# K and Q of a sliding-window attention: masked while they leave PSUM, or copied first and masked in place

## The chip, the cores and the metric

The kernel runs on one core of a Trainium2 chip. The metric is the device time of one execution in microseconds. Five engines work from queues of their own: PE (TensorE) multiplies, DVE (VectorE), ACT (ScalarE) and POOL (GpSimd) do the elementwise work, and SP issues nearly all DMAs. They wait for each other through semaphores.

## The reference, cut to what matters

Two kinds of block run twice in turn on x of 2048 rows by 512 columns: attention with 32 heads of 16 columns and a window of 256 rows, and an MLP over the rows.

```python
def _A_ref(x, wqkv, wo):            
    q, k, v = ...                   # x @ wqkv, split into heads
    scores = einsum("bhqd,bhkd->bhqk", q, k) * (Dh ** -0.5)
    mask = (idx[:, None] - idx[None, :] >= 0) & (idx[:, None] - idx[None, :] < W)
    scores = where(mask, scores, -1e9)
    p = softmax(scores)
    return einsum("bhqk,bhkd->bhqd", p, v)... @ wo

def _B_ref(x, w1, b1, w2, b2):
    u = gelu(einsum("bsd,sf->bdf", layernorm(x), w1) + b1)
    return transpose(einsum("bdf,fs->bds", u, w2) + b2)

x = x + _A_ref(layernorm(x), ...); x = x + _B_ref(layernorm(x), ...)   # twice
```

## The kernel before

**Work.** A layer's attention goes through four blocks Q of 512 rows. For each block and each group t of 128 columns (8 heads), `project` (L521 to L530) makes K, Q and V: four 128x512 matmuls into one PSUM bank. Each (Q, t) then has nine steps m. A step is a score product (L684, cells of 64x64 in PE), an exp on ACT that writes the weights P to `p_sb` (L695), products with `edge` that mask the window's ends in P (L712, on DVE or POOL), and the product with V (`emit_pv`, L733) some steps later. There are 288 steps in the two layers. The MLP is two large products, L855 (u) and L928 (y); parts of both are placed among the attention steps.

**Masks of K and Q.** The score product works on several heads at once, so K and Q are kept in two copies each, with rows of other heads set to zero. K goes to `k_sb` with the two copies interleaved in runs of 32 columns, by the two-column mask `half`; Q goes to `q_sb` as two copies of 512 columns by `even`. `masked` (L532 to L544) does this straight from the bank: on DVE as one product of 1024 columns (L537), whose inputs are the bank in PSUM and the mask in SBUF, or on ACT as two activations with a scale (L542). The bank is held until this is done. The very first K and Q (t = 0 of the first block) come in halves of 256 columns (`first_half`), each masked in the same way.

**V.** V is copied out of its bank (L358 or L360), transposed (L601) and spread into `v_all` by a product of two SBUF operands (L586, on DVE, POOL or ACT). LayerNorm is L460 to L494, the inverse of the softmax sums L759 to L765, their spreading L777, the output product L653.

**Order.** Nothing is scheduled when the kernel runs. The program makes 2537 operations, each with the engines that could do it and a cost in ns. `ORDER` (L28) then gives, for each engine, the list of operations that it performs, in order, each named by two letters that number the operations as they are made. `BANKS` gives the one of two PSUM banks, 6 and 7, that each of the 200 "misc" products uses: projections, output products, parts of u and y. `Plan.needs` works out which semaphores each operation waits for. Each engine goes through its list strictly, so an operation that waits holds all behind it.

**Start.** SP loads x, the weights of K and Q in quarters, and V's weights. PE first multiplies an identity by itself as a warm-up (`warm`, L446: one operation is ten 128x128 matmuls, `WARM` = 10 operations), six of them at once, one after the first two transposes, three among the first scores.

Of the kernel before, what the change touches and what calls it, by code (L numbers as in the profile page):

```python
# [10 lines left out]
P = 128  # L11
# [3 lines left out]
WARM = 10  # L15
# [14 lines left out]
AuAvAwAxAyAzBLBJA0BPBRBNBTBXBVDTB1CeCuA1A2CjCoBpCyCcC3C9D1A3CnDEDKCxBtC2DODXC8DkDDDeDJDNDmDVDbBxDsDxB5DBD4DiD9DrGsEKECDwEFFZD3EPD8EBEaEJGQEOETEjEeEyEp  # L30
EuGiE3EiE8EoEtFBE2FJE7FOF2FVFAFIFcFEFxFNFSF4HlF9FbGCFwGIF1F8GMGBGTHYGdGHGLGSGWGlICGpGvHLG2GkGoG9G7HCGuG1HGIQHOG5HBHFHVHNHSHeHaHiHrI0HyHdH6HhHqHxH-HuII
H5H+INKmIcIHIMIgIkIoIVIsKUIxIfIjI6JpI-IrIwJVH1JaI5I+JiJCJmJEJuJZJ1JfJyJ6JdKwJlJ+JtJxKLJ5LpKPJ9KXLbKhKKKOKpMFKtKWKaKzK-K6KoLBKsKyK5LGLPLKK9LFLSNILYLJLh
NSLmLRLVLuNLL1LgL9LlLdMCLtL0MKL8MBLxMJMOMPMdNBMlMhMWMpNwMtMgMkMxL4M5MsMwM+NgNEM4M9NNNQNXNDNdMSNKNnNUNtNaN1NcNmN5OOOGNsN0OKO+OTN4OFOJOeOQOXOiOnOpOhOtPm
O0OmO6NqPBOsOzPFM0O5PKPSQYPAPEPfPJPPPZPVPtPYPePjPNP4PyNkPcQAPiPsQHPoPxP3QRP-O3QGQbQKQVQoQkQUQaQfRXP7QvQeQ1Q-Q5QjQuQ0RDORRKQ4Q+RORHQERURcRRRNRhRTRbRgRm
RlRzR0QsSuR3R4R5SxSyS0SrS1SvS3SwSGS6S7SDS4S2SVSJSsSRSNS8S5StSlSmSzSnS9TRTFTBTNTSTHTDTOTdTVThTZTaTeTWSoTiSpSqS-TLTJT1TwT7T2T8UAUBTxUpUOUdUXUZUqUTUVUkU2
UbUeU6UlUiVbUPVMVCVKWdVVVQWeU+VeVjYXVGYYVoVvVUVsXyXzWiVdV0ViV4VnVuVzWAWNV9WPV3V-WHWEWyXRWZWUXAWlWLWqZgXBWvW3WTWYWkXkYrW8WpXNWuZWXWW2W7XGXbX7XgXVXaXfXp
YQXuX4aFYAXoYFXtZvYMX3X-YEYJYTaGYmYta2YyYSYlY3YqYxY8adZHZAa3Y2Y7Y-ZZZGZKZRbgZdZjZEbhZqZxZYcDZ2ZcZiZpZ6Zta-aCaNZ-Z1aaZ5aBaKaWaQaqaVaZajaia8apaxaSa7aybK
cGbFbdcHbZbEbJbSdRbqbucbbybNbcb7blcAambtbxcTb6b-cYdjcgcFcXckatcscdcweNc4cjcrc8bmdJcvc3c7dIdNdMdUb1eZdedmcndTdXdrczdxd4d9dld-dqdwd3eEgAeId7eQemeWeDeHef
duejePeTerfDeze7eeebeifAfIeqeyeufNe6e-fbfHfMfUfffjfngjfrfvfegXf3fifqfuf9e2gDf2gIiDgQf8gCgHgNgUh0gcgggLgogTgbgfgsfQg5gngrg9hchIg4hTfyg8hEhMhXheighChihp
hshthWhwh3hbhhhFh7hohviAiSiIh2h6iPhGiWh-iFiaiTikiOiVipiLiZivijioi3iuidi2i-i+jCjJjQjNkRjTjXjgj4jcjojMiyjujSjWjbjyjnjtjxj8jkj3kDkAkHjlkKkOkWi7kGkbkNkVka  # L40
kgkfktkui8kLkxkykzlrlslulolllmlvlplAl0lxk9l1lylPltlDlzlLlHl2lwlqlnlflglhmBl9l-mLl3mMmbmTmUmHl7mImcmPmQlimXljlkmYl5mFmDmjm1msmkmnmwmom2mxmtm5m6nCm+m-nH
# [13 lines left out]
AjAiBMBQBSBUBYAtB2CfAmArCkCpCzAsC4C+CdDFDLBuDPDYDfDnDcByDtDyB6D+D5GtEDELB8EQEbEkEUEVEqEvE4E9FCFKFPFWFdFFFyF5F+GDGJGNGUGeGmGqGwG3G+HDHHHPHWHfHjHsHzH7IA
IJIOIdIhIpItIyI7JAJWA4JbJjJnJvJzJhJ7J-KMKQKYKiKqKuK0K7LCLHLLLTLZLiLnLvL2L+MDMLMQMeMiMqMuMyM6M-NFNONYNeNoNuN2N6OHOLOUOfOjOqOuO1O7PCPGM1PTPLPgPaPuPkPzP5
# [214 lines left out]
def bass_interleave_layers__sliding_block__mixer_token_mlp__prompt_kernel(  # L271
# [23 lines left out]
    with es:  # L295
# [49 lines left out]
        def dve(fn, work, prio, **kw):  # L345
            return plan.op({DVE: (work, fn)}, prio=prio, **kw)
# [716 lines left out]
```

## Time and profile before

| | |
|---|---|
| median of 3 runs | 492.03 us (491.97 to 492.04) |
| the profiled execution | 492.09 us |
| its span, first to last instruction | 490.3 us |
| granted TensorE clock | 1.00 |
| first exp | 12.2 us |
| matmuls of warm-up | 100 |
| ACT's idle time that ended with a score product | 23.8 us in 47 waits |
| POOL's idle time that ended with an exp | 99.0 us in 65 waits |

The page gives the busy time of each engine, the chain of work that ended last (followed back from the last instruction to whatever released each one), and groups of equal instructions: line, engine, operation, output and inputs, shape, count, then total busy us and mean ns, then idle time before them and what ended it. A line of the chain has its start, its duration and the instruction. Neighbouring instructions of one engine overlap a little, so two durations may add to more than the time that passes.

### The profile page before, as it was taken

How to read it: one execution, taken by the hardware profiler on the slowest of the kernel's cores; microseconds unless marked ns; L12 is line 12 of the kernel's file. 1: busy time of each engine (PE TensorE's matmuls, PEld its weight loads, DVE VectorE, ACT ScalarE, POOL GpSimd, SP SyncE). 2: the span in 40 equal slices, each digit the busy share in tenths (PEclk: the TensorE clock that was granted, in tenths of full speed). 3: DMA queues.
4: the chain of work that ended last, by engine and by line, in shares of the span. 5: the costliest groups of instructions: out<-in, count | busy, mean ns of one | idle time of the engine just before them, and what ended most of it. 6: DMA issues, size and time to landing. Idle time of an engine off the chain costs nothing.

```text
span 490.3 us, 17141 instructions
## 1 busy us (share of the span) xinstructions
PE 467.3 (95%) x7614; PEld 255.4 (52%) x7706; DVE 337.4 (69%) x710; ACT 319.8 (65%) x391; POOL 196.3 (40%) x362
## 2 busy tenths in 40 slices
PE   8989989999999999999999999999999999999997
PEld 6544555565555444444455555655556544444444
DVE  7999988988878550256878677999978745220214
ACT  5989989999989202404769898989999830440000
POOL 4989886444622210021439253645674220000000
DMA  7533159200105872240116300240020666080833
GB/s 215 100 77 90 40 115 97 70 6 25 50 6 153 237 175 76 75 132 19 31 16 170 51 27 4 39 101 8 24 70 4 197 188 171 0 226 19 228 107 118
DMA packets 83465, 43.58 MB, mean 89 GB/s; under 512 B 18752, under 2 KB 82368, under 8 KB 83392
## 3 DMA queue, kind: packets, MB, share of 16 engines
q1 hardware_dynamic: 79520, 42.48, 33.1%
q0 software_dynamic: 3872, 0.02, 1.8%
q8 instruction: 60, 0.98, 0.9%
q14 instruction: 13, 0.11, 0.1%
HBM read 32.51 MB, written 2.10 MB: 71 GB/s over the span
## 4 chain that ended last, share of the span: by engine, by line
PE 77%; DVE 14%; ACT 4%; issue 3%; POOL 1%; POOLq 0%
PE ps L855 19%; PE ps L928 18%; PE ps L526 12%; PE ps L684 11%; PE ps L733 9%; PE ps L653 4%; ACT p_sb L695 4%; DVE q_sb L537 2%; DVE stats L460 2%; DVE p_sb L712 2%; PE ps L777 1%; DVE v_all L586 1%; DVE x_sb L657 1%; DVE k_sb L537 1%; DVE oU L358 1%
## 5 line engine op out<-in xcount | busy, mean ns | idle before, releaser
L695 ACT ACTIVATE p_sb<-ps 128x1024 bf16<-128x1024 f32 (+8 forms) x288 | 260.8, 973 | 26.0 <-PE ps L684 23.8
L712 POOL TENSOR_TENSOR p_sb<-p_sb,edge 128x128 bf16<-128x128 bf16 (+2 forms) x225 | 107.5, 494 | 122.8 <-ACT p_sb L695 99.0
L684 PE MATMUL ps<-q_sb,k_sb 64*64 64x288 bf16 (+8 forms) x2816 | 106.4, 250 | 2.3 <-issue 1.3
L526 PE MATMUL ps<-xhT,wqkv 128*128 128x512 bf16 x335 | 86.2, 380 | 7.7 <-issue 4.7
L733 PE MATMUL ps<-p_sb,v_all 64*64 64x288 bf16 (+8 forms) x2816 | 89.5, 246 | 1.7 <-DVE oU L358 0.7
L684 PEld LDWEIGHTS ps<-q_sb,k_sb 64*64 64x64 bf16 x2816 | 53.1, 106 | 51.8 <-ACT p_sb L695 32.7
L733 PEld LDWEIGHTS ps<-p_sb,v_all 64*64 64x64 bf16 x2816 | 58.7, 107 | 15.4 <-issue 4.7
L928 PE MATMUL ps<-uT,w1buf 128*128 128x512 bf16 x270 | 62.6, 379 | 1.2 <-issue 0.8
L932 DVE SCALAR_TENSOR_TENSOR x_sb<-ps,b2col,x_sb 128x512 bf16<-128x512 f32 x31 | 22.2, 745 | 50.8 <-PE ps L928 50.7
L712 DVE TENSOR_TENSOR p_sb<-p_sb,edge 128x64 bf16<-128x64 bf16 (+2 forms) x175 | 44.4, 272 | 12.7 <-ACT p_sb L695 12.0
L526 PEld LDWEIGHTS ps<-xhT,wqkv 128*128 128x128 bf16 x376 | 30.5, 97 | 40.0 <-issue 5.6
L855 PE MATMUL ps<-xh_sb,w1buf 128*128 128x512 bf16 x175 | 43.4, 380 | 2.1 <-issue 1.3
L928 PEld LDWEIGHTS ps<-uT,w1buf 128*128 128x128 bf16 x280 | 26.6, 98 | 32.4 <-issue 1.1
L492 ACT ACTIVATE xh_sb<-x_sb,shift,rstd 128x512 bf16<-128x512 bf16 x9 | 7.1, 811 | 54.8 <-POOL shift L486 54.8
L460 DVE BATCH_NORM_STATS2 stats<-x_sb 128x6 f32<-128x512 bf16 x64 | 42.3, 680 | 0.3
L482 POOL TENSOR_TENSOR rstd<-vare,mhalf 128x4 f32<-128x4 f32 x15 | 15.7, 1047 | 54.4 <-DVE nmean L484 32.7
L537 DVE TENSOR_TENSOR q_sb<-ps,even 128x1024 bf16<-128x1024 f32 x30 | 36.4, 1214 | 1.3 <-PE ps L526 1.0
L537 DVE TENSOR_TENSOR k_sb<-ps,half 128x1024 bf16<-128x1024 f32 (+1 forms) x27 | 32.3, 1198 | 4.8 <-PE ps L526 3.5
L928 PE MATMUL ps<-uT,oU 128*128 128x512 bf16 x149 | 34.9, 379 | 0.3
L653 PE MATMUL ps<-wo_sb,oT 128*128 128x512 bf16 x114 | 30.1, 380 | 1.6 <-issue 1.0
L855 PE MATMUL ps<-xh_sb,k_sb 128*128 128x512 bf16 x125 | 29.6, 379 | 0.2
L855 PEld LDWEIGHTS ps<-xh_sb,w1buf 128*128 128x128 bf16 x192 | 17.1, 98 | 21.2 <-issue 2.4
(87 smaller groups left out, 457.8 us busy)
## 6 DMA issues: line engine op xcount, KB each, us to landing
w1buf<-in_B_w_dram SPq DMA_DIRECT2D x10, 896.0 KB
oU<-in_B_w_dram SPq DMA_DIRECT2D x6, 896.0 KB
w1buf<-in_B_w_dram SPq DMA_DIRECT2D x10, 512.0 KB
oU<-o SPq DMA_DIRECT2D x16, 256.0 KB
k_sb<-in_B_w_dram SPq DMA_DIRECT2D x16, 256.0 KB
xhT<-in_B_w_dram SPq DMA_DIRECT2D x8, 256.0 KB
q_sb<-in_B_w_dram SPq DMA_DIRECT2D x8, 256.0 KB
out_dram<-x_sb SPq DMA_DIRECT2D x15, 128.0 KB
```

Of the source, the lines that this page charges most:

```text
L460: dve(lambda e: e.bn_stats(stats[:, t, :], x_sb[:, t, :]), 690, prio, reads=[R("x", t)], writes=[R("stats", t)])
L482: pool(lambda e: e.tensor_tensor(rstd[:, sl], vare[:, sl], mhalf[:], op=ALU.pow), 1000, prio, reads=[R("vare", g), R("mhalf")], writes=[R( ...
L526: last = e.matmul(ps[:, b, :], lhsT=wqkv[:, c, c0:c0 + P], rhs=xhT[:, buf, c, :], start=(c == 0), stop=(c == 3))
L537: return e.tensor_tensor(dst, src.unsqueeze(2).to_broadcast([P, n, 2, w]), mask[:].unsqueeze(1).unsqueeze(3).to_broadcast([P, n, 2, w]), o ...
L653: last = e.matmul(ps[:, b, :], lhsT=oT[:, buf, t, i * P:(i + 1) * P], rhs=wo_sb[:, t, :], start=(t == 0), stop=(t == 3))
L684: last = e.matmul(ps[64 * c:64 * c + 64, 2 * half + r, 32 * i0:32 * i1], lhsT=k_sb[rows, ring, t, kb % 16, :], rhs=q_sb[rows, t, c, 32 * i ...
L695: latest[0] = plan.op({ACT: (170 + int(2 * (512 - c0) * 0.84), lambda e: e.activation(p_sb[:, slot, :, c0:512], ps[:, 2 * half:2 * half + ...
L712: return e.tensor_tensor(v, v, g, op=ALU.mult)
L733: last = e.matmul(ps[64 * r:64 * r + 64, B_O + (c ^ r), 32 * i0:32 * i1], lhsT=v_all[rows, col:col + 64], rhs=p_sb[rows, slot, r, 32 * i0: ...
L855: r = e.matmul(ps[:, b, :], lhsT=blk[:, n, (ft % 2) * P:(ft % 2 + 1) * P], rhs=xh_sb[:, 4 * g + n, :], start=(first and g == quarters[0] a ...
L928: r = e.matmul(ps[:, b, :], lhsT=blk[:, fc, (st % 2) * P:(st % 2 + 1) * P], rhs=uT[:, fc, :], start=(fc == 0), stop=(fc == NFT - 1))
L932: dve(lambda e: e.scalar_tensor_tensor(x_sb[:, st, :], ps[:, b, :], b2col[:, st:st + 1], x_sb[:, st, :], op0=ALU.add, op1=ALU.add), 750, prio,
```

## The change

`job_k` and `job_q` no longer call `masked` but a new `masked_late`. It copies the bank as it is into one of the two copies in SBUF (one plain copy of 512 columns, DVE or ACT), and a second operation then multiplies that copy in place with a pattern: it reads the copy twice (as a broadcast), multiplies with `rows`, a widened form of `half` and `even` made once at the start, and writes both copies. That product has both inputs in SBUF, in bfloat16, and may be done by DVE or POOL. The bank is held by the plain copy alone. `first_half` keeps the old form.

```diff
-WARM = 10
+WARM = 8
...
+        rows = sb("rows", [P, 2, 2, 32])
+        for n, m in enumerate((half, even)):
+            dve(lambda e, n=n, m=m: e.tensor_copy(rows[:, n], m[:].unsqueeze(2).to_broadcast([P, 2, 32])), 80, -98,
+                reads=[R(("half", "even")[n])], writes=[R("rows")])
...
+        def masked_late(b, prio, dst, src, pattern, key, writes):
+
+            copy_out(dst[:, :, 1], src, b, prio, 680, writes)
+
+            def twice(e):
+                return e.tensor_tensor(pattern[0], pattern[1], pattern[2], op=ALU.mult)
+            plan.op({DVE: (690, twice), POOL: (2110, twice)}, reads=[R(key)], writes=writes, prio=prio)
...
         def job_k(Q, t, prio):
 
             b, ring = project(Q, 1, D + t * P, prio), Q % 2
-            masked(b, prio, k_sb[:, ring, t].rearrange("p k (h n) -> p k h n", h=2), ps[:, b, :].rearrange("p (k n) -> p k n", n=32),
-                   half, "half", [R("k", ring, t, h) for h in range(2)])
+            dst = k_sb[:, ring, t].rearrange("p k (h n) -> p k h n", h=2)
+            masked_late(b, prio, dst, ps[:, b, :].rearrange("p (k n) -> p k n", n=32),
+                        (dst, dst[:, :, 1].unsqueeze(2).to_broadcast([P, 16, 2, 32]), rows[:, 0].unsqueeze(1).to_broadcast([P, 16, 2, 32])),
+                        "rows", [R("k", ring, t, h) for h in range(2)])
...
         def job_q(Q, t, prio):
 
             b = project(Q, 0, t * P, prio)
-            masked(b, prio, q_sb[:, t].unsqueeze(1), ps[:, b, :].unsqueeze(1), even, "even", [R("q", t, c) for c in range(2)])
+            dst = q_sb[:, t].rearrange("p c (g n) -> p c g n", n=32)
+            masked_late(b, prio, q_sb[:, t].unsqueeze(1), ps[:, b, :].unsqueeze(1),
+                        (dst, dst[:, 1].unsqueeze(1).to_broadcast([P, 2, 16, 32]), rows[:, 1].unsqueeze(2).to_broadcast([P, 2, 16, 32])),
+                        "rows", [R("q", t, c) for c in range(2)])
```

All five lists of `ORDER` and the list of `BANKS` are new; they were searched with a model of how DMAs queue. Decoded, they give the operations to engines as follows (only rows that differ):

| operation | before | after |
|---|---|---|
| K and Q out of the bank (62) | DVE 56, ACT 6 | DVE 42, ACT 20 |
| second product of K and Q (62) | none | DVE 53, POOL 9 |
| warm-ups on PE | 10 | 8 |
| V spread (L586, L591) | DVE 26, ACT 3, POOL 11 | DVE 32, ACT 1, POOL 7 |
| normalisation (L489, L492) | DVE 20, ACT 9, POOL 31 | DVE 25, ACT 6, POOL 29 |
| edge masks (L712) | DVE 175, POOL 225 | DVE 179, POOL 221 |
| V copy | DVE 23, ACT 9 | DVE 22, ACT 10 |
| copies of the PV banks | DVE 54, ACT 10 | DVE 53, ACT 11 |
| copies of parts of u | DVE 8, ACT 4 | DVE 9, ACT 3 |
| inverse (L761, L764) | DVE 6, ACT 3, POOL 7 | DVE 9, ACT 2, POOL 5 |
| ones beside V, V's weights turned | ACT 6, POOL 24 | DVE 1, ACT 6, POOL 23 |

SP's first nine loads stood in the order x (four tiles in three loads), K's weights first quarter, x (next four tiles), Q's first, Q's second, V's weights, K's second. They now stand: x (four tiles in three loads), Q's first, V's weights, x (next four), K's first, Q's second, K's second. On PE, five warm-ups stand at the start, two behind the first two transposes and one among the first scores. After the first half projections PE makes a Q and a V projection ahead of the first scores; before it made a Q projection.

## The prediction

> **What bounds the kernel now.** I read the page first, for the engines and for the chain of work that ended last.
>
> ```profile
> PE 467.3 (95%) x7614; PEld 255.4 (52%) x7706; DVE 337.4 (69%) x710; ACT 319.8 (65%) x391; POOL 196.3 (40%) x362
> PE 77%; DVE 14%; ACT 4%; issue 3%; POOL 1%; POOLq 0%
> ```
>
> PE is on the chain for three quarters of the time, but a busy PE need not be at its peak, so I asked for the busy time by stage: start and first quarter of attention 1, rest of it, the MLP between the layers, attention 2, the last MLP. The columns are PE, PEld, DVE, ACT, POOL.
>
> ```profile
> 12.00:45.00 33.00, 30.47 (x516) 16.08 (x518) 32.62 (x73) 30.99 (x47) 30.05 (x66) 1.00 0.47 99
> 45.00:140.00 95.00, 88.98 (x2264) 53.22 (x2292) 86.73 (x177) 90.48 (x100) 57.47 (x103) 1.00 0.30 52
> 140.00:260.00 120.00, 117.99 (x1230) 58.81 (x1242) 68.39 (x147) 55.30 (x75) 28.09 (x46) 1.00 0.35 94
> 260.00:375.00 115.00, 109.41 (x2555) 64.37 (x2580) 96.71 (x192) 105.74 (x123) 66.48 (x117) 1.00 0.22 53
> 375.00:490.30 115.30, 110.61 (x959) 54.78 (x974) 43.41 (x90) 30.12 (x38) 9.19 (x15) 1.00 0.48 134
> ```
>
> The two MLP stretches (235 us) are PE's alone; nothing in this change makes them shorter. DVE limits 12 to 45 us (32.6 of 33.0), ACT the rest of attention 1 (90.5 of 95) and attention 2 (105.7 of 115). The change works where DVE, ACT and PE are all within some 8% of full, so a gain on one is soon capped by the next.
>
> **Durations.** From the groups by shape:
>
> ```profile
> L537 DVE TENSOR_TENSOR q_sb<-ps,even 128x1024 bf16<-128x1024 f32 x30 | 36.4, 1214 | 1.3 <-PE ps L526 1.0
> L537 DVE TENSOR_TENSOR k_sb<-ps,half 128x1024 bf16<-128x1024 f32 x26 | 31.7, 1218 | 4.8 <-PE ps L526 3.5 <-PE ps L684 1.1
> L358 DVE CAST vT<-ps 128x512 bf16<-128x512 f32 x23 | 15.7, 683 | 2.1 <-PE ps L526 1.8
> L360 ACT ACTIVATE vT<-ps 128x512 bf16<-128x512 f32 x9 | 5.5, 609 | 4.8 <-PE ps L526 4.8
> L542 ACT ACTIVATE k_sb<-ps,half 128x512 bf16<-128x512 f32 x10 | 6.3, 692 | 1.2 <-PE ps L526 1.2
> L586 DVE TENSOR_TENSOR v_all<-vB,v_all 128x1024 bf16<-128x1024 bf16 x16 | 11.9, 745 | 0.0
> L586 POOL TENSOR_TENSOR v_all<-vB,v_all 128x1024 bf16<-128x1024 bf16 x5 | 10.7, 2149 | 8.5 <-DVE vB L601 8.5
> ```
>
> The new copy is the vT copy (DVE 683 ns, ACT 609). The new product, bf16 from SBUF with a broadcast operand, is nearest to V's spreading at L586 (DVE 745, POOL 2149). In a full DVE queue each instruction starts some 75 ns before the last ends (40.58, then 41.72 behind a 1.21 us product), so what it takes from the queue is 1.14 for the old masked copy, and 0.61 each for the new copy and an undisturbed new product.
>
> **The change, part by part.** Counts are from the decoded tables.
>
> *K and Q on the engines.* DVE had 56 of the 62 masked copies: 56 x 1.14 = 63.8 us. It gets 42 copies and 53 products: 95 x 0.61 = 58.0, and if the products stretch as L586 does (745 against 0.67 undisturbed) 53 x 0.075 = 4 more. ACT had 6 in two instructions each (12 x 0.69 = 8.3) and gets 20 copies (20 x 0.61 = 12.2). POOL gets 9 products, 19.3. The tables also move other work: DVE gains 6 V spreads, 5 normalisations, 4 edge masks and three small steps of the inverse, together about 9 us; ACT loses 2 spreads and 3 normalisations, about 5 us. Net: DVE 58 + 4 - 63.8 + 9 = +7 us, ACT about -0.5, POOL about +9. DVE is on the chain for 14% of 490.3 = 69 us of its 337 us, one fifth; I charge a fifth of its 7 us: **+1.4**. Bounds: 0 if it all lies beside PE and ACT, +7 if DVE is the limit throughout. ACT's and POOL's changes I cost at nothing, since POOL is idle 28 to 49 us of each attention stretch; without that cover POOL's 9 us would fall on the weights P that PV reads.
>
> *The bank.* It comes free after 0.68 (or 0.61 on ACT) instead of 1.22 us. In the chain of waits the masked copy stands 14 times. In two places PE's next projection waited for it:
>
> ```profile
> 288.67 1.24 DVE k_sb L537
> ...
> 326.47 1.15 DVE q_sb L537
> 327.62 0.08 issue
> 327.70 0.81 PE ps L526 x3
> ```
>
> In the others the next piece is DVE's own queue, which is in the last term. 2 x (1.14 - 0.61) = **-1.1**; what is late next is the exp chain, which takes any more. Bounds 0 and -3.
>
> *Two warm-ups fewer.* In the old order three of ten stand behind the first projections, in the new one one of eight. The chain holds them as work (1.12 us for two, 0.56 for one):
>
> ```profile
> 13.35 1.12 PE ps L446 x20
> ```
>
> Two gone: **-1.1** (0 if another engine limits there). Of the group before the data comes, 60 matmuls become 50; PE then waits for the first transpose anyway (0.65 us idle, now 1.2).
> The Trainium skill ("TensorE: Matmul & The Clock Gate", What's actually happening) says that about 3.4 us of idling brings PE back to half rate. Here the pace of the warm-ups goes from 107 to 56 ns at 4.4 us. By that rule the gap of 1.2 us costs nothing.
>
> *The loads.* On SP's queue the first K weights move from 4th to 7th of nine loads, behind V's weights. POOL's wait for V's weights, the 8th, ended at 11.6 us with 2.3 of 2.56 MB issued up to it; the bytes up to the 7th are 2.05 MB, so I estimate 10.4 for the K weights, while the first half product of K now starts at 8.46. Three halves (0.27 each), a Q projection and a V projection (0.9 each) then stand ahead of the first scores, which come at about 13.0 instead of 11.8; but that V projection is work done early (0.97). Left: 0.3 to 1.2, I take **+0.5**.
>
> *The order.* It is new everywhere, and no row shows it. From the tables I added PE's work between a bank's product and the bank's next user, and took off the eviction's time: margins under 0.5 us go from 30 to 23 of 198 places, at K's and Q's products from 12 to 8. The fewest scores between a K or Q projection and its first use go from 2 (three times) to 3 (once). I take 0.3 us for each of the 7 tight places, **-2.1**. Bounds: ACT waited for scores 47 times, 23.8 us in all, 0.5 each; ten waits fewer or ten more are -5 and +5.
>
> **The sum.** +1.4 - 1.1 - 1.1 + 0.5 - 2.1 = -2.4. The profiled execution took 492.09 us (span 490.3 and 1.8 around it), the runs' median is 492.03: 492.03 - 2.4 = **489.6**.
>
> **Rivals.**
>
> *POOL and DVE hold each other up (slower).* The old K and Q products have one operand in PSUM and one in SBUF; their 30 durations for Q lie between 1181 and 1225 ns, whatever POOL does. Products with both operands in SBUF do not keep their time:
>
> ```profile
> 38.97 1.09 DVE L586 TENSOR_TENSOR v_all<-vB,v_all 128x1024 bf16<-128x1024 bf16 x1
> 44.80 0.68 DVE L586 TENSOR_TENSOR v_all<-vB,v_all 128x1024 bf16<-128x1024 bf16 x1
> 260.63 0.65 DVE L712 TENSOR_TENSOR p_sb<-p_sb,edge 128x128 bf16<-128x128 bf16 x1
> ```
> ```profile
> 38.90 0.62 POOL L428 CAST v_all<-even 128x512 bf16<-128x512 f32 x1
> 259.07 2.13 POOL L586 TENSOR_TENSOR v_all<-vB,v_all 128x1024 bf16<-128x1024 bf16 x1
> ```
>
> The first DVE product seems to begin in earnest when POOL's cast ends (39.52); the edge mask at 260.63, of a kind that took 0.22 at 47.24, ends 0.08 after POOL's product (261.20). The change makes 53 more such products on DVE and 9 on POOL of 2.15 us. If half of the 53 meet POOL (busy 60% of attention) at 0.41 each and each of the 9 holds one edge mask for 0.43, that is 11 + 4 = 15 us of DVE; with half of it on the path, 7.5, less the 1 or so already charged: about **496**. It decides when over a quarter of the products meet POOL while DVE is full. Against it: the 16 long spreads average 745, only 60 ns over an ordinary one. Chance 0.20.
> The Trainium skill ("SBUF — State Buffer", Who interferes with whom) states this as a rule: a DVE instruction with two SBUF inputs and a GpSimd one that reads SBUF exclude each other, and the later waits for the whole of the earlier. The trace agrees in the places above, and by that rule the full 15 us would be DVE's and the sum 496.
>
> *K and Q come too late (slower).* Two instructions and a second wait in a queue: 0.61 + 0.61 and two waits of about 1.1 are 3.4 us against a lead of 3 to 5 scores of 1 us each; on POOL 1.5 more. Half a microsecond at each of six such places, and the order's gain halved: about **494**. For it: the tightest leads; against: mean lead 15 scores. Chance 0.12. PE going cold at the start, by the 27 slow warm-ups (1.5 us more than fast ones), would be 493.5; chance 0.02.
>
> *Nothing comes of it (no change).* ACT is 95% and 92% busy in the stretches it limits and its work stays (-0.5), so PE's time turns into waiting for exp: **491.8**, chance 0.14.
>
> *The order brings more (faster).* Ten waits of ACT fewer, -5 instead of -2.1: **486.5**, chance 0.16. My forecast has the remaining 0.36.
>
> **How the numbers follow.** About 0.2% (1 us) is what a measurement of this kernel can tell from no change. Faster: 0.36 + 0.16 = 0.52; same 0.14; slower 0.20 + 0.12 + 0.02 = 0.34. The range goes from the order's good end, 485, to just past the first rival, 497.
>
> **What would show it.** Two-operand products near 680 to 750 ns and copies near 680 and 610; no K or Q copy on the chain ahead of a projection; only ten warm-up matmuls after the first scores; first exp near 13 us. DVE busy some 345 us, ACT 319, POOL 205. Wrong if the new products average over 900 ns, or POOL's edge masks stretch with them (rival one), if scores wait for DVE or POOL at k_sb or q_sb (rival two), or if ACT's wait for scores stays near 24 us (no change).

## The result and the profile after

The changed kernel took 499.98 us in the median of 5 runs (498.35 to 500.56) beside 492.03 for the kernel before; the ratio is 1.016, with a 95% interval of 1.0139 to 1.0181. It is 8 us slower, where 2.4 us less were forecast. The profiled execution is the fastest of the five: 498.35 us, span 496.5, granted clock 1.00. The other four take 1.4 to 2.2 us more, so small differences below are read both from the medians and from the traces.

The page of the kernel after, engines and chain:

```profile
PE 480.9 (97%) x7686; PEld 255.6 (51%) x7686; DVE 351.2 (71%) x769; ACT 320.8 (65%) x392; POOL 219.7 (44%) x358
PE 72%; DVE 13%; DMA 5%; POOL 4%; ACT 3%; issue 2%; SPq 1%; POOLq 0%; DVEq 0%
```

DVE has 13.8 us more than before, POOL 23.4, ACT 1. PE's share of the chain fell from 77 to 72%, and DMAs, which were not in the chain at all, hold 5%. (PE's own busy time is no guide here: matmul records are missing in some traces, and unchanged PE work reads 467 or 481.)

The busy time by stage, with the bounds that were used for before; columns PE, PEld, DVE, ACT, POOL, then clock, DMA share, GB/s:

```profile
12.00:45.00 33.00, 29.87 (x473) 14.35 (x475) 32.45 (x76) 30.18 (x47) 30.03 (x60) 1.00 0.33 83
45.00:140.00 95.00, 90.37 (x2264) 52.34 (x2256) 87.91 (x187) 87.84 (x97) 67.17 (x103) 1.00 0.38 44
260.00:375.00 115.00, 113.75 (x2485) 63.58 (x2486) 101.36 (x225) 105.13 (x123) 71.61 (x110) 1.00 0.20 53
```

In 45 to 140 us ACT falls from 90.5 to 87.8: the engine that limited this stage now idles 7.2 instead of 4.5 us of it. POOL rises from 57.5 to 67.2.

The groups by shape, after (busy us, mean ns of one, then idle before):

```profile
L558 DVE TENSOR_TENSOR q_sb<-q_sb,rows 128x1024 bf16<-128x1024 bf16 x28 | 22.8, 814 | 2.6 <-ACT q_sb L362 2.5
L558 DVE TENSOR_TENSOR k_sb<-k_sb,rows 128x1024 bf16<-128x1024 bf16 x25 | 20.0, 808 | 0.0
L360 DVE CAST k_sb<-ps 128x512 bf16<-128x512 f32 x20 | 13.5, 677 | 1.0 <-PE ps L533 0.8
L362 ACT ACTIVATE k_sb<-ps 128x512 bf16<-128x512 f32 x11 | 6.6, 601 | 7.0 <-PE ps L533 6.8
L558 POOL TENSOR_TENSOR k_sb<-k_sb,rows 128x1024 bf16<-128x1024 bf16 x6 | 13.4, 2225 | 6.3 <-ACT k_sb L362 6.3
L732 POOL TENSOR_TENSOR p_sb<-p_sb,edge 128x256 bf16<-128x256 bf16 x82 | 58.3, 719 | 38.5 <-ACT p_sb L715 38.4
```

The copies cost what their rows of before said (677 and 601 ns). The products average 811 ns, and POOL's widest edge mask went from 678 to 719; its row in before:

```profile
L712 POOL TENSOR_TENSOR p_sb<-p_sb,edge 128x256 bf16<-128x256 bf16 x85 | 56.8, 678 | 64.9 <-ACT p_sb L695 64.4
```

**Where in the run the time is lost.** ACT's 288 exps are the same work in both kernels. The table gives how much later the n-th exp begins than in before's trace, in us; 0 to 143 are attention 1, 144 to 287 attention 2. It is worked out from the starts of the exps in each trace; the last column is the end of DVE's last instruction, behind which only DMAs are left.

| profiled run | exp 0 | 9 | 21 | 54 | 72 | 143 | 144 | 287 | end |
|---|---|---|---|---|---|---|---|---|---|
| after | 2.7 | 3.0 | 0.0 | 1.2 | 3.8 | 5.0 | 6.1 | 5.1 | 6.4 |
| e1 copy and product, old lists | 0.8 | 0.8 | 1.9 | 4.5 | 4.7 | 6.2 | 6.2 | 12.5 | 12.5 |
| e5 old kernel, more DVE work | 0.4 | 0.6 | 1.3 | 1.8 | 2.4 | 3.1 | 3.1 | 5.0 | 5.0 |
| e20 e1 with half products | 0.5 | 0.5 | 0.3 | 1.6 | 1.6 | 1.9 | 1.9 | 4.7 | 4.7 |
| e9 after, bias loads at 60 us | 2.8 | 2.9 | -0.2 | 5.8 | 6.5 | 8.2 | 9.4 | 8.3 | 9.3 |
| e10 after, edges early | 1.7 | 1.5 | -1.5 | -0.3 | 2.0 | 2.8 | 4.0 | 3.0 | 4.7 |
| e15 after, b2col later | 3.2 | 3.4 | 0.4 | 1.6 | 2.9 | 5.4 | 6.6 | 5.6 | 6.6 |
| e16 both mends | 3.1 | 2.9 | -0.2 | 1.0 | 1.9 | 4.1 | 5.3 | 4.2 | 5.4 |
| e18 e16 with half products | 1.5 | 1.3 | -2.3 | -2.1 | -1.1 | 0.2 | 1.4 | -0.2 | 1.3 |

After is 3.0 us late at exp 9 and level with before at exp 21. From there it loses 5.0 us up to the end of attention 1; the two MLP stretches add 1.1 and 1.3, and attention 2 gives 1.0 back. The gain between exp 9 and 21 is 3.0 to 3.6 us in each of the table's runs with the new lists, however late it starts. A gain of 1.2 us lies there in the old kernel too when it loses the two warm-ups (e19, below); the rest of it was not taken apart.

### The profile page after: what moved, and what is told of

Read it like the earlier page. It is cut to its first block, busy times and chain, and to the rows that moved or that the text cites. A ratio compares the mean times of both kernels' runs of the same rounds, so it can differ in the third digit from the quotient of the medians.

```text
span 496.5 us, 17280 instructions
## 1 busy us (share of the span) xinstructions
PE 480.9 (97%) x7686; PEld 255.6 (51%) x7686; DVE 351.2 (71%) x769; ACT 320.8 (65%) x392; POOL 219.7 (44%) x358
## 4 chain that ended last, share of the span: by engine, by line
PE 72%; DVE 13%; DMA 5%; POOL 4%; ACT 3%; issue 2%; SPq 1%; POOLq 0%; DVEq 0%
PE ps L948 18%; PE ps L875 17%; PE ps L533 11%; PE ps L704 10%; PE ps L753 9%; PE ps L673 5%; ACT p_sb L715 3%; DMA oU<-o 2%; DMA den_c<-o 2%; DVE p_sb L732 1%; POOL p_sb L732 1%; DVE stats L467 1%; DMA den_c<-oU 1%; DVE v_all L606 1%; PE ps L797 1%
## 5 line engine op out<-in xcount | busy, mean ns | idle before, releaser
L715 ACT ACTIVATE p_sb<-ps 128x1024 bf16<-128x1024 f32 (+7 forms) x288 | 262.3, 974 | 23.8 <-PE ps L704 19.7
L732 POOL TENSOR_TENSOR p_sb<-p_sb,edge 128x256 bf16<-128x256 bf16 (+2 forms) x221 | 115.8, 538 | 87.9 <-ACT p_sb L715 82.3
L533 PE MATMUL ps<-xhT,wqkv 128*128 128x512 bf16 x376 | 95.4, 381 | 0.4 <-DVE vT L360 0.3
L948 PE MATMUL ps<-uT,w1buf 128*128 128x512 bf16 x280 | 64.1, 379 | 0.1
L732 DVE TENSOR_TENSOR p_sb<-p_sb,edge 128x64 bf16<-128x64 bf16 (+2 forms) x179 | 51.8, 303 | 10.8 <-ACT p_sb L715 7.2
L489 POOL TENSOR_TENSOR rstd<-vare,mhalf 128x4 f32<-128x4 f32 x15 | 16.0, 1068 | 91.6 <-DVE nmean L491 49.3
L875 PE MATMUL ps<-xh_sb,w1buf 128*128 128x512 bf16 x192 | 46.0, 380 | 0.1
L499 ACT ACTIVATE xh_sb<-x_sb,shift,rstd 128x512 bf16<-128x512 bf16 x6 | 4.8, 811 | 49.6 <-POOL shift L493 49.6
L673 PE MATMUL ps<-wo_sb,oT 128*128 128x512 bf16 x128 | 32.1, 381 | 0.0
L920 DVE TENSOR_TENSOR v_all<-v_all,ps 128x512 f32<-128x512 f32 x12 | 8.2, 688 | 27.6 <-PE ps L875 27.6
L677 DVE TENSOR_TENSOR x_sb<-x_sb,ps 128x512 bf16<-128x512 bf16 x32 | 21.7, 680 | 7.9 <-PE ps L673 7.9
```

The costliest lines, as they stand in the source:

```text
L489: pool(lambda e: e.tensor_tensor(rstd[:, sl], vare[:, sl], mhalf[:], op=ALU.pow), 1000, prio, reads=[R("vare", g), R("mhalf")], writes=[R( ...
L533: last = e.matmul(ps[:, b, :], lhsT=wqkv[:, c, c0:c0 + P], rhs=xhT[:, buf, c, :], start=(c == 0), stop=(c == 3))
L673: last = e.matmul(ps[:, b, :], lhsT=oT[:, buf, t, i * P:(i + 1) * P], rhs=wo_sb[:, t, :], start=(t == 0), stop=(t == 3))
L677: dve(lambda e: e.tensor_tensor(x_sb[:, tile, :], x_sb[:, tile, :], ps[:, b, :], op=ALU.add), 680, prio, reads=[R("x", tile)], shares=[BK( ...
L715: latest[0] = plan.op({ACT: (170 + int(2 * (512 - c0) * 0.84), lambda e: e.activation(p_sb[:, slot, :, c0:512], ps[:, 2 * half:2 * half + ...
L732: return e.tensor_tensor(v, v, g, op=ALU.mult)
```

## The experiments

The theories that the expectations number: 1, POOL and DVE hold each other up (the prediction's first rival); 2, the new order of DMAs; 3, the rest of the new order; 4, DVE has no room, and each us of work added there costs about half a us. D is the bias packets, S and R the start, O that the new order is bound elsewhere than by DVE.

### Second products without the new lists

e1 puts the new form into the kernel before, with its old lists. Each of DVE's 56 K and Q copies is followed at once by its product; ACT's six keep the old form.

```diff
-            masked(b, prio, q_sb[:, t].unsqueeze(1), ps[:, b, :].unsqueeze(1), even, "even", ...)
+            masked_late(b, prio, q_sb[:, t].unsqueeze(1), ps[:, b, :].unsqueeze(1), (...), "rows", ..., 0)
```

> The old lists, banks and warm-ups; only the 56 masked copies of K and Q on DVE become a plain copy and, right behind it on DVE, the in-place product (the 6 on ACT stay as they were). Theory 1, POOL and DVE hold each other up in products with two SBUF operands: the 56 products average 0.80 us or more, DVE's excess grows by 8 us or more, time 496 to 500. Theory 2, the new order of DMAs on SP is to blame (softmax sums and output halves wait behind weights): SP's list is the old one, so 491 to 494. Theory 3, the rest of the new order: 491 to 494 too.

Measured: 504.54 us (503.97 to 505.34), ratio 1.0237 [1.0221, 1.0252], DVE 356.7 us busy. Worse than any theory had it: 11.6 us for 19.3 us of DVE, 0.60 per us.

e2, e3 and e4 are e1, before and after with POOL's edge masks as fills, which read nothing in SBUF. POOL's masking is left out in them.

```diff
-    plan.op({DVE: (90 + 2 * w * k, f), POOL: (190 + int(3.75 * w * k), f)},
+    plan.op({DVE: (90 + 2 * w * k, f), POOL: (190 + int(3.75 * w * k), z)},   # z: e.memset(p_sb[...], 0.5), in parts
```

> As the split in the old order, but POOL's edge masks only write (short fills of about the same length in all, over the same elements; the window's edges in P are then not masked, so that part of the computation is left out). Theory 1: products fall to about 0.70 us and the time comes within 1.5 us of the unsplit kernel with the same fills. Theories 2 and 3 say nothing of this pair: it stays as far apart as the split and the kernel before.

> The kernel before with POOL's edge masks as fills that only write (the edges on POOL are left unmasked). Theory 1: DVE loses most of the 9.5 us by which its edge masks run over, and the time falls a little, 488 to 491. Theories 2 and 3: POOL was not on the path, 491 to 493.

> The changed kernel with POOL's edge masks as fills that only write (the edges on POOL are left unmasked). Theory 1: at least two thirds of the loss goes, 489 to 493, within 2 us of the kernel before with the same fills. Theory 2, DMAs: the loss stays, 496 to 499. Theory 3: the loss stays.

Measured: e2 499.71, ratio 1.0142 [1.0124, 1.016]; e3 490.87, 0.9957 [0.9942, 0.9972]; e4 498.0, 1.01 [1.0084, 1.0115], beside 492.98. The same edit gives 4.8 us in e1, 2.1 in before, and in after 2.0 by the medians and 3 by the ratios (1.016 - 1.010). So the part of the hold-up that lies between POOL's edge masks and the second products is worth 2.7 us in the old lists (4.8 - 2.1) and 0 to 1 in the new ones. It is real and it is not the main thing: theory 1's own figures (e2 within 1.5 us of e3, e4 at 489 to 493) are missed by 7 and 5 us. In DVE's busy time the fills are worth 11.0 us in e1, 5.1 in before and 7.0 in after. They do not take all of the hold-up away: in e2 K's products still average 835 ns (886 in e1). POOL's spreads, casts and normalisations still read SBUF in these runs; nothing was tried for those.

### What a us of DVE work costs

e5 is the kernel before with 56 added reductions, one behind each masked copy, of one SBUF input, so not of the kind that rival one is about.

```diff
+        def more_work():
+            plan.op({DVE: (240, lambda e: e.tensor_reduce(idle[:, n:n + 1], tri[:], axis=mybir.AxisListType.X, op=ALU.add))}, ...)
```

> The old kernel whole, with 56 more instructions on DVE, one behind each masked copy of K or Q: a sum over 128 constant columns, one SBUF input, into a scratch column that nothing reads. About 0.15 us of DVE each, 8 us in all. Theory 4, DVE's queue as a whole sets the time (the four runs before moved by about 0.6 us for each us of DVE's busy time): plus 5 us, 496 to 499. By DVE's share of the chain, as the prediction had it, a fifth: plus 1.6, 493.5 to 495. Theory 1 in its narrow form (only products with two SBUF inputs cost): under 2.

Measured: 496.8 (495.07 to 497.13), ratio 1.0087 [1.0063, 1.0112]. From its page and its groups:

```profile
PE 481.5 (97%) x7706; PEld 256.5 (52%) x7706; DVE 347.3 (70%) x766; ACT 320.4 (65%) x391; POOL 197.0 (40%) x362
L565 DVE TENSOR_REDUCE idle<-tri 128x1 f32<-128x128 bf16 x56 | 15.3, 273 | 0.0
```

DVE grew by 9.9 us (337.4 to 347.3) and the time by 4.65: 0.47 us per us. A fifth, as its share of the chain would have it, is 2.0. Theory 4 holds for the old lists, with no POOL in it.

e6 leaves one of the two copies of K and Q unwritten by the second product, in the kernel after; e20 does the same in e1.

```diff
-(dst, dst[:, 1].unsqueeze(1).to_broadcast([P, 2, 16, 32]), rows[:, 1].unsqueeze(2).to_broadcast([P, 2, 16, 32]))
+(dst[:, 0], dst[:, 1], rows[:, 1, 0].unsqueeze(1).to_broadcast([P, 16, 32]))
```

> The changed kernel whose second product writes only one of the two copies, 512 columns instead of 1024; the other copy keeps the other heads' rows, so that part of the mask is left out. DVE gives up some 20 us and POOL 9. Theory 4: minus 10 to 13 us against the change, 486 to 490, below the kernel before. By the chain's fifth: minus 4, 494 to 497. Theories 2 and 3 (DMAs, order): minus 2 or less.

> The old lists with copy and second product (504.5 us beside 493.0), the second product over one of the two copies only, so some 17 us less on DVE; the other copy stays unwritten. In the mended new order the same cut gave 3.2 us for 17.5 us of DVE (0.18 us per us), while 9.9 us more of it cost 4.65 us in the old order (0.47). Theory 4 (the old lists have no room, so every us of DVE costs half): 494.5 to 497. If a second product's price is the same in both orders: 500.5 to 502.

Measured: e6 496.13 (494.93 to 500.13), ratio 1.0095 [1.0061, 1.0129]; DVE at 333.0 us is below before's 337.4, yet the kernel stays 4 us slower. It gains 3.9 us on after for 18.2 us of DVE, 0.21 per us; theory 4's 486 to 490 is missed. e20: 497.17 (496.04 to 498.63), ratio 1.0094 [1.0074, 1.0114]; 7.4 us less than e1 for 13.2 us of DVE (356.7 to 343.5), 0.56 per us. In the old lists theory 4 holds again; in the new ones something else is in the way.

### Whether the early release of the bank is worth anything

e8 is the kernel after, but the 42 K and Q that DVE takes are masked in one product straight from the bank, as before; their second products are gone.

```diff
+            if len(plan.base) in on_vector():
+                masked(b, prio, dst, src, half if which == 1 else even, ...)
+                return
```

> The new order; the 42 K and Q that DVE copies are masked in one product as before (1.14 us of DVE) and their second products are dropped, 34 on DVE and 8 on POOL; the 20 that ACT copies keep both steps. DVE gives up about 5 us in all (42 x 0.54 more, 34 x 0.75 and some stretch less). Theory 4: minus 3 us against the change, 495 to 498. Theory 3 (the rest of the order is at fault): 498 to 501. Theory 1 in its narrow form: two thirds of the new loss gone, 493 to 495.

Measured: 504.12 (502.52 to 504.43), ratio 1.0236 [1.0207, 1.0265]: 4 us slower than after, with 5 us less on DVE and 26 less on POOL, and slower than any theory had it. ACT's wait for scores rises from 19.7 to 25.1 us, and the chain of e8 has `DVE k_sb` and `DVE q_sb` at 2.8% each. PE's projections wait for these products; in after no matmul of a projection waits for a copy or a product of K or Q:

```profile
PE ps L541 <- DVE q_sb L552: 1.8, 4, 0.7
PE ps L541 <- DVE k_sb L552: 0.9, 3, 0.3
```

The new lists count on the bank after 0.6 us, and these waits are 2.7 of the 4 us. The rest need not be the bank: at the place of a copy of 0.6 us DVE now works 1.2, which also delays what stands behind it. That part of the change works as it is meant to.

### The start

In after, q's first masked half waits behind two constants of 32x32. From the timeline of after, DVE, then POOL beside it:

```profile
11.68 1.49 DVE L412 TENSOR_SCALAR edge<-tri 32x32 bf16<-32x32 bf16 x1
13.20 0.52 DVE L412 TENSOR_SCALAR edge<-tri 32x32 bf16<-32x32 bf16 x1
13.64 0.21 DVE L422 CAST v_all<-even 128x128 bf16<-128x128 f32 x1
13.78 0.67 DVE L544 TENSOR_TENSOR q_sb<-ps,even 128x512 bf16<-128x512 f32 x1
```

```profile
11.63 0.61 POOL L435 CAST v_all<-even 128x512 bf16<-128x512 f32 x1
12.19 0.95 POOL L990 MEMSET spread<- 128x1024 bf16 x1
13.09 0.61 POOL L435 CAST v_all<-even 128x512 bf16<-128x512 f32 x1
```

The first ends at 13.17, where POOL's memset ends (13.14), the second at 13.72, where POOL's cast ends (13.70). The same instruction at 7.41 took 0.16 us. PE is done with its projections at 13.50 and then waits for q:

```profile
11.61 1.89 PE L533 MATMUL ps<-xhT,wqkv 128*128 128x512 bf16 x8
14.50 0.62 PE L704 MATMUL ps<-q_sb,k_sb 64*64 64x288 bf16 x16 [1.00 <-DVE q_sb L544]
```

e10 moves three such instructions to 6.0 to 6.5 us, where POOL is idle:

```diff
 DVE's list of after
+    edge<-tri x3          ahead of the first normalisation
     ... statistics, normalisation ...
-    edge<-tri             ahead of the first xhT copy
     ...
-    edge<-tri x2          ahead of the first half of q
```

> The kernel after with one edit: three small DVE instructions of the constants (edge<-tri), of which two took 2.04 us at 11.68 beside POOL's cast and memset and held up q's first masked half, stand at about 6.3 us of DVE's list. Theory S (the late start, first exp 14.95 against 12.23 us, is carried to the end): first exp near 13.0 and 498.0 to 498.5 us. Theory R (the start is regained by exp 18, where after stood only 0.7 us behind before, since ACT and PE wait there for other things anyway): first exp near 13.0 and 499.5 to 500.3 us.

Measured: 496.73 (496.43 to 497.71), ratio 1.0095 [1.0078, 1.0113]: 3.2 us less than after by the medians, 1.9 by the profiled executions (498.35 and 496.48). The table shows why: e10 is ahead of after by 1.0 us at the first exp, 1.5 at exp 9, and by 1.5 to 2.2 ever after. Theory R (the start is regained) falls. That after is level with before at exp 21 is a gain of its own, which e10 has too (3.0 us between exp 9 and 21); it is not the start being made up. Theory S has the direction, not the figures: the first exp comes at 13.97, not near 13.0, and the time is below its 498.0.

Not all of the lateness is mended: the cast that now stood there, `v_all<-even`, took 1.53 us at 11.66 instead of 0.21, again until POOL's memset was done at 13.12.

### DMAs

> The changed kernel with SP's old list of DMAs, loads at the start included. Theory 2 (the new DMA order makes output halves and softmax sums wait): half of the loss or more comes back, 492 to 496. Theory 4: within 2 us of the change, 498 to 502.

e7 gives SP its old list in the kernel after. Measured: 536.46 (534.62 to 537.75), ratio 1.0898 [1.0863, 1.0932]; the chain has `DMA w1buf<-in_B_w_dram` at 4.8%. The lists fit each other, and one old list among new ones is no test of theory 2.

The chain of after showed a DMA piece that looked like a cause:

```profile
79.38 0.59 DVE k_sb L360
79.97 0.04 issue
80.02 5.71 DMA den_c<-o
85.73 0.02 issue
85.75 0.61 ACT o L362
86.36 0.04 issue
86.41 0.65 PE ps L753 x20
```

POOL issues b2col's load, 2048 elements of 4 bytes, at 78.46, and the softmax sums queue behind it. The windows of after there:

```profile
80.00:82.00 2.00, 2.00 (x60) 1.16 (x56) 1.88 (x5) 2.00 (x4) 0.00 (x0) 1.00 2.86 319
82.00:84.00 2.00, 2.00 (x31) 1.05 (x24) 2.00 (x4) 1.88 (x2) 1.89 (x4) 1.00 5.50 37
84.00:86.00 2.00, 0.73 (x14) 0.23 (x12) 2.00 (x4) 0.24 (x1) 2.00 (x2) 1.00 2.33 72
```

The DMA share rises from 2.86 to 5.50 while the bytes fall from 319 to 37 GB/s; in 84 to 86 PE is busy 0.73 and ACT 0.24 of 2 us. Four runs move these loads: e9 both to 60 us in after, e15 b2col alone to 87.0 us in after, e12 both into a gap in before, e13 b2col into a clash in before.

```diff
 POOL's list of after (e15)
     edge mask
-    load of b2col
     edge mask x3, second product of q, edge mask
+    load of b2col
     edge mask
```

> The kernel after with one edit: the two bias loads that POOL issues (b1col, b2col, some 3,840 packets of four bytes) stand together near 60 us of POOL's list, between two rounds of softmax sums, where the kernel after issues b2col at 78.46 us and its packets fill the DMA engines from 80 to 86 us (DMA share 2.86 and 5.50 in 80:82 and 82:84) while den_c<-o, issued at 80.02, waits 5.71 us behind them. Theory D (the new order put these packets ahead of a softmax sum; ACT idles 1.87 us and PE 1.68 us for it, and part of the 1.2 to 3.8 us step between exp 54 and 72 is this): 496.5 to 498.5 us, and no piece of den_c<-o over 2 us in the chain of waits near 80. Theory 4 (only the added DVE work sets the time; what PE loses there it would lose to DVE a moment later): 499.5 to 500.5.

> The kernel after with one edit: only b2col's load goes, in POOL's list, from 78.46 us to about 86.7 us, where POOL idles 1.76 us and no softmax sum is in flight (the next is at 93). In the earlier try both bias loads stood at 60 us: the step between exp 54 and 72 fell from 2.6 to 0.7 us, but POOL's edge masks came 2.6 us later at 61 to 65, PE ran short and its clock fell to 0.71 in 65:70, and 4.6 us were lost ahead of exp 54. Theory D (the packets cost what ACT and PE idle behind den_c<-o, 1.9 us): 497.5 to 498.5 us, exp 72 near 2 us behind before. If that wait only moves: 499.5 to 500.5.

> The kernel before with one edit: both bias loads stand at about 96 us of POOL's list, in a gap between two rounds of softmax sums, instead of at 70 and 72, right ahead of den_c<-o at 72.5. It is the control of the run with the bias loads moved in the kernel after. Theory D: before pays little there (no den_c piece in its chain of waits), so 491.0 to 492.2; a gain over 1.5 us would say that the bias loads cost both kernels the same and explain no difference.

> The kernel before with one edit: b2col's load (2,048 packets of four bytes) stands at about 91 us of POOL's list, behind den_c<-oU and ahead of oU<-o and two den_c<-o at 92 to 94 us, as the kernel after has it ahead of one den_c<-o at 80. POOL idles there, so only the DMAs differ. Theory D: the softmax sums land 4 to 6 us later, and the time grows by 1 to 3 us, to 493 to 495. If such a wait is hidden anyway: 491.7 to 492.3.

Measured: e9 501.29 (500.98 to 503.24), ratio 1.0193 [1.0172, 1.0215]. The step between exp 54 and 72 falls from 2.6 to 0.7 us, but 4.6 us were lost ahead of it. The windows of e9:

```profile
60.00:65.00 5.00, 3.24 (x99) 1.85 (x88) 4.68 (x9) 5.00 (x6) 4.67 (x8) 1.00 1.20 15
65.00:70.00 5.00, 2.46 (x72) 2.19 (x72) 4.69 (x10) 0.48 (x1) 1.20 (x2) 0.71 0.05 3
```

Two issues of 1.32 and 1.15 us on POOL, put where POOL had edge masks to do, left ACT 0.48 of 5 us busy, and PE's clock fell to 0.71. That POOL's delay set this off is the reading of these two rows, not a test of its own.

e15: 498.15 (497.97 to 498.54), ratio 1.0115 [1.0102, 1.0128]. That is what theory D expected (497.5 to 498.5). The medians say 2 us less than after, and the two intervals do not meet (1.0139 to 1.0181 for after). The profiled executions say none (498.54 and 498.35); they are the slowest of e15's four and the fastest of after's five. The windows of e15 show the piece mended, and the rows behind them ACT's wait for the sum, in after and in e15:

```profile
82.00:84.00 2.00, 2.00 (x46) 1.27 (x43) 2.00 (x4) 2.00 (x3) 1.51 (x3) 1.00 1.62 79
84.00:86.00 2.00, 1.53 (x35) 0.85 (x38) 2.00 (x4) 1.39 (x3) 2.00 (x2) 1.00 0.37 69
```

```profile
85.75 0.60 ACT L362 ACTIVATE o<-ps 128x512 f32<-128x512 f32 x1 [1.87 <-DMA den_c<-o]
```

```profile
84.88 0.60 ACT L362 ACTIVATE o<-ps 128x512 f32<-128x512 f32 x1 [0.61 <-DMA den_c<-o]
```

The step from exp 54 to 72 is 1.3 instead of 2.6 us, and from 72 to 143 2.5 instead of 1.2: in the trace the gain is given back. From exp 9 to the end e15 loses 3.2 us, after 3.4. e12, 491.96, ratio 1.0002 [0.9984, 1.0019], moves nothing in before, so the loads are no cost that both kernels share. e13, 492.07, 1.001 [0.9993, 1.0027], tells nothing: its clash was too weak to make a wait. The packets were through by 95 us (DMA share 2.10 in 93:95, 0.04 after it), and the sums' reciprocal began at 96.33 us, no later than before's (96.86). So the longest DMA piece of the chain is worth 2 us by the medians and close to nothing between the two traces, where DVE, busy 5.88 of the 6 us around it in after, is the likely next to come late; which of the two holds stays open. The other long DMA pieces of after's chain (5.11 us at 154.46, 4.18 at 401.65 and 4.39 at 405.85) were not tried.

### The mends together

e16 is e15 with DVE's constants early, the cast included; e17 adds the fills of e4 (POOL's masking left out); e18 is e16 with the half product of e6 (one copy unwritten). In their texts "the run before" is e15 for e16, and e16 for e17.

> The run before with a second edit: the three edge<-tri and DVE's v_all<-even cast (1.53 us at 11.66 in the run with the edges early, again beside POOL's cast and memset) stand at about 6.3 us of DVE's list. Theory S (what the start loses is carried to the end): first exp 0.3 to 1.0 us behind before, against 2.7 in after; with b2col moved 494 to 496 us. If the cast's 1.3 us are made up later: 495.5 to 497.

> The run before with POOL's edge masks as fills that read nothing (the masking itself is left out on POOL). The fills gave 2.0 us in the kernel after and 2.1 in before. If the three costs are separate they add: 492 to 494 us, level with or just behind before (492.0), which does 12 us less on DVE; against before with the same fills (490.9) 1 to 3 us would be left as the price of the second products. If more than 5 us are left, the price sits in them.

> The run with start and b2col mended, and the second product over one of the two copies only (512 of 1,024 columns; the other copy stays unwritten), which took 18 us off DVE and 16 off POOL and gave 3.9 us in the kernel after, where a late start and a cold PE lay in the same run. Theory 4 (about half a us of time per us of DVE work): 486 to 489 us. Theory O (the new order is bound elsewhere, and DVE's load is not what costs): 491 to 495.

Measured: e16 497.04 (495.34 to 500.92), ratio 1.0095 [1.0065, 1.0124]; e17 496.56 (496.26 to 499.68), 1.008 [1.0067, 1.0093]; e18 493.84 (493.01 to 496.34), 1.0031 [1.0017, 1.0045]. The gains do not add: e16 is no better than e10 alone, and the fills give 0.5 us where 2 more were looked for. Beside before with the same fills (490.87) e17 is still 5.7 us longer; its expectation puts what is left beyond 5 into the second products. In its trace e16 starts 3.1 us late despite its mend, for another reason. POOL's first piece of V's weights, in the timelines of after and of e16:

```profile
7.89 0.39 POOL L444 COPY wqkv<-w1buf 128x256 bf16<-128x256 bf16 x1
```

```profile
9.47 0.39 POOL L444 COPY wqkv<-w1buf 128x256 bf16<-128x256 bf16 x1 [1.01 <-DMA w1buf<-in_A_wqkv_dram]
```

That load was issued at 2.69 us in e16 and landed 6.72 later; e15's landed after 6.08. The new lists put V's weights fifth of nine loads and their copies ahead of POOL's and ACT's other work, so a late landing holds both engines. In before that copy waits 2.87 us for its load and comes at 11.61, and the first exp does not depend on it:

```profile
11.61 0.40 POOL L437 COPY wqkv<-w1buf 128x256 bf16<-128x256 bf16 x1 [2.87 <-DMA w1buf<-in_A_wqkv_dram]
```

e18 loses nothing on balance after its start (1.3 us at exp 9, 1.3 at the end), where e16 loses 2.5 (2.9 to 5.4). So half of the second products, 17.5 us of DVE (350.3 to 332.8) and 15.5 of POOL, is worth 2.5 us by the traces and 3.2 by the medians: 0.14 to 0.18 per us of DVE. That is theory O's range, not theory 4's: the rate of 0.5 holds in the old lists and not in the new ones. The table shows where they differ. From exp 21 to 143 the half is worth 1.8 us in the new lists (4.3 in e16, 2.5 in e18) and 2.7 in the old ones (4.3 in e1, 1.6 in e20). In attention 2 it is worth 0.5 and 3.5: there the new lists seem to have room for it. That they have it because they were searched with this work in them was not tested.

### Two warm-ups fewer, alone

```diff
-WARM = 10
+WARM = 8
 PE's list of before: without the 9th and the 10th warm-up
```

> The kernel before without the two warm-ups of ten products that the change drops (they stand behind the second scores, half of the 1.12 us at 13.35, and behind the ninth scores near 18 us); all else is as before. The prediction charged them at -1.1 us, since PE stood in the chain of waits there: 491.0 to 491.4. If ACT's exps set the time there, or DVE's first products: 491.8 to 492.6. If PE goes cold without them: 493 to 494.

Measured: 491.82 (490.94 to 493.32), ratio 0.9984 [0.9973, 0.9995], or -0.8 us [-1.3, -0.2]. It is the only complete kernel here whose interval lies below before. Its trace is 1.2 us ahead at exp 54 and 0.2 at the end.

## Why the prediction was wrong, by its own steps

- **Durations and copies**: right (683 and 609 forecast, 677 and 601 measured).
- **K and Q on the engines, +1.4**: the size failed, and the price that was put on it had no ground. DVE's growth was 13.8 us, not 7, and POOL's 23.4, not 9. Worked out from the traces as time over the shortest fifth of each kind of instruction, the stretching grew from 18.3 to 33.4 us on DVE, 15.1 more, and on POOL from 7.6 to 23.3. The price was a fifth, DVE's share of time on the chain of before. In the lists from which it was read a us of DVE cost 0.47 to 0.60 (e5, e20, e1). In the new ones the halved products put it at 0.14 to 0.21 (e6, e18), so a fifth comes near there by luck; it is no constant either, for the fills, which change POOL too, give 0.28 to 0.43 in after and about 0.1 in e16. With the right size and the price of the halves the term would be +2 to +3 (13.8 x 0.14 to 0.21), an estimate. POOL's idle time was misread too, as 28 to 49 us of each attention stretch: the rows give 37.5 and 48.5 in the two long ones and 3.0 in 12 to 45.
- **The bank, -1.1**: right in sign. In lists that count on the early release its loss brings 2.7 us of waits, and 4 us in all (e8).
- **Two warm-ups, -1.1**: near, -0.8 by e19's ratio, though its median lies 0.4 us above the range that was expected of it. The gap of 1.2 us ahead of the first transpose was 0.20, since the 50 warm-ups at the start took 5.41 us where 60 took 4.93 in before. It cost nothing, as forecast: the transposes begin at 7.04 and in before at 7.03.
- **The loads, +0.5, first exp near 13**: the step that failed most plainly. K's weights landed at 10.3 as estimated (10.4), but the first scores came at 14.50, not 13.0, and the first exp at 14.95. PE's own work was done at 13.50, 1.7 us later than before's scores where 1.2 were estimated; the other 1.0 is PE's wait for q on DVE. The step counted only PE's matmuls ahead of the first scores and not what stands ahead of the first q on DVE, two small constants held up beside POOL. The first exp is 2.7 us late, and e10, which takes 1.0 to 1.5 of it away, shows that what the start loses is carried to the end.
- **The order, -2.1**: the tight places were about right and did not matter. ACT's wait for scores fell from 23.8 to 19.7 us, and the kernel got slower: ACT now waits for other things (2.8 us for V's weights, 1.9 for a softmax sum, neither of which ACT waits for in before's trace). Fewer waits at tight places are not time by themselves. The bound of +5 stood in the range but not among the rivals: no case of a worse order had a price.
- **MLP stretches**: "nothing in this change makes them shorter" was no reason that they stay as long. They lose 2.4 us in the trace of after, of which attention 2 gives 1.0 back. In the first PE takes the same 74.25 us from the last score of attention 1 to the first of attention 2, though the new lists have one projection more there. What differs is ACT: in after it copies a q behind that first score, and the table load ahead of the exp (`ACT_TABLE_LOAD`, 1.28 us) stands behind that copy; in before the table load starts 0.34 us ahead of the score. After, then before:

```profile
237.05 0.60 ACT L362 ACTIVATE q_sb<-ps 128x512 bf16<-128x512 f32 x1 [0.27 <-PE ps L533]
237.67 1.28 ACT L715 ACT_TABLE_LOAD   x1
238.96 0.97 ACT L715 ACTIVATE p_sb<-ps 128x960 bf16<-128x960 f32 x1
```

```profile
231.41 1.28 ACT L456 ACT_TABLE_LOAD   x1
232.81 0.95 ACT L695 ACTIVATE p_sb<-ps 128x960 bf16<-128x960 f32 x1
```

The scores of that exp begin at 236.95 and 231.75, so it starts 2.0 us behind them instead of 1.1. Behind attention 2 the new lists hold two PV products more, and in the last MLP weights go into a buffer of K, and PE waits for them, a wait that before's trace does not have:

```profile
PE ps L875 <- DMA k_sb<-in_B_w_dram: 1.5, 1, 1.5
```

- **Rival one, 496**: the mechanism is there, and its second sign too: POOL's edge masks stretch (their part of POOL's 15.7 us is 10.6). That DVE's 15.1 us meet the 15 that were worked out is in part luck: 7.1 of them lie in the new products, for 11, and 5.3 in DVE's edge masks, for 4. In after's timeline, DVE's product and POOL's:

```profile
289.59 2.61 DVE L558 TENSOR_TENSOR q_sb<-q_sb,rows 128x1024 bf16<-128x1024 bf16 x1
292.12 0.68 DVE L558 TENSOR_TENSOR k_sb<-k_sb,rows 128x1024 bf16<-128x1024 bf16 x1
```

```profile
289.37 2.28 POOL L558 TENSOR_TENSOR k_sb<-k_sb,rows 128x1024 bf16<-128x1024 bf16 x1
```

DVE's first product starts 0.22 us after POOL's, which ends at 291.65; it ends 0.55 later, and the next one, with no POOL product beside it, takes 0.68 in all. The Trainium skill ("SBUF — State Buffer", Who interferes with whom) says that of such a pair the later one waits for the whole of the earlier. These rows agree to about 0.1 us. But half of the 15 us on the path is not borne out: taking away POOL's reads at the edge masks gave after 2 to 3 us and before 2.1, so 1 at most is due to the change there; for POOL's other instructions it wasn't tried.
- **Rival two, 494**: did not happen; scores waited for no late product of K or Q beyond 0.5 us.
- **Small slips**: -5 instead of -2.1 makes 486.7, not 486.5, and 27 warm-ups at 107 instead of 56 ns are 1.4 us, not 1.5.

By the traces the forecast missed by 8.7 us (-2.4 against 498.35 - 492.09 = +6.3). By terms the start is off by 2.2 (2.7 for 0.5), the engines by 0.5 to 1.5, and the MLP stretches net of attention 2 by 1.4. By places, nothing is lost up to exp 21, where the late start and the gain behind it cancel; 6.4 us are lost behind it, where the forecast had +1.4 - 1.1 - 2.1 = -1.8. Of the 5.0 us between exp 21 and the end of attention 1, halving the second products takes 1.8 (e16 and e18). What makes the rest of these 5.0, and why the order's -2.1 does not show there, is not settled, nor are the 1.6 us between the median of after and its profiled run. What a late landing of V's weights does to the start was seen in two traces (e15, e16) and not tried alone.

## What to carry to other kernels

An engine's share of the chain is not the price of more work on it: DVE work cost 0.5 to 0.6 us per us in lists made without it and about 0.2 in lists made with it, so price added work by a run that adds some. Follow a new order at the start instruction by instruction on every engine, small constants and first loads too, since what is lost there is carried to the end. A long DMA piece on the chain is a place to test, not a cost: mending this one, of 5.71 us, gave 2 us by the medians and nothing between two traces.

## What the runs showed of the hardware that was not expected

Tiny DVE instructions with one SBUF input are held up too: two 32x32 ones took 1.49 and 0.52 us beside POOL's casts and memset (0.16 each elsewhere) and ended within 0.03 us of a POOL instruction, and a 128x128 cast took 1.53 instead of 0.21. The Trainium skill (the same section) says that casts and tensor_scalar can run in a two-port mode, in which they and POOL exclude each other for a whole instruction; the rows agree with the exclusion, and which mode these ran in no row shows.

b2col's load, 8 KB of 4-byte elements, raised the DMA share to 5.50 and held an 8 KB softmax sum for 5.71 us, where the same load in the gap of e15 raised it to 1.21 (88 to 90 us) and landed 3.9 instead of 7.6 us after its issue. ACT's idle time for the sum fell from 1.87 to 0.61 us in e15, and the traced time did not fall.
